# One-hot preparation in pinned half steps, comparisons on other slots, and a sum moved to ScalarE, in an FNet and PEER kernel

## The chip, the cores and the metric

The kernel runs on one core of a Trainium2 chip. A core has a matmul engine (TensorE, PE in the profile), three engines for elementwise work (VectorE or DVE, ScalarE or ACT, GpSimd or POOL), and SyncE (SP), whose queue issues most of the DMA transfers here. The metric is the device time of one launch in microseconds (us), the median of several runs.

## The reference

The reference normalizes the rows of `x` (2048 tokens of 512 numbers), and adds to `x` two functions of the normalized `xn`: a real-valued 2D Fourier transform, and a mixture of tiny experts (PEER) with 32 heads, of which each picks 2 of 4096 experts for each token.

```python
a = jnp.einsum("bsd,ed->bse", x, dft_hid_re)
b = jnp.einsum("bsd,ed->bse", x, dft_hid_im)
y = jnp.einsum("ts,bse->bte", dft_seq_re, a) - jnp.einsum("ts,bse->bte", dft_seq_im, b)
...
s1 = jnp.einsum("nhd,ed->nhe", q1, k1)          # q1, q2: halves of xf @ w_q
s2 = jnp.einsum("nhd,ed->nhe", q2, k2)
i1 = jnp.argsort(-s1, axis=-1)[..., :K]         # K = 2, E = 64
i2 = jnp.argsort(-s2, axis=-1)[..., :K]
...
eidx = (i1[..., :, None] * E + i2[..., None, :]).reshape(BS, H, K * K)
...                                             # best 2 of the 4 candidates: top_s, top_e
g = _softmax(top_s, axis=-1)
ue = u[top_e]
ve = v[top_e]
act = _gelu(jnp.einsum("nd,nhkd->nhk", xf, ue))
out = jnp.einsum("nhk,nhk,nhkd->nd", g, act, ve)
...
return x + _A_ref(xn, ...) + _B_ref(xn, ...)
```

## The kernel before

The first 406 us hold the Fourier transform, the scores of the heads and their routing (the two best keys of each half, the gates). The change touches nothing of that. The DFT matrices are inputs, and the kernel uses their symmetry; so it also checks in passing that the matrices given have it. The second part works on all 4096 experts, without a gather, for 16 blocks of 128 tokens. For each block `b` there are four kinds of work:

- `z`: the matmuls of `xn` with all rows of `u`. Two blocks at a time are computed by a scheme in the manner of Strassen (28 slots of matmuls, L1186), for which VectorE adds partial results out of PSUM (L1227, L1235, L1238) and ScalarE copies others and applies the gelu (L1215), into the block's `act`. Four PSUM banks (`z`) rotate; TensorE waits for an add when it needs the bank. A z phase has 16 slots of the plan (below). The matrices of the scheme come in part from a ring of loads `s` (L1169).
- `g`: the gates spread to a 128 x 4096 table, as matmuls of one-hot matrices (`g_mm`). A step `g{b}_{tg}` (four to a block) has two halves of 16 matmuls of 128x32 (L1289). Each half needs an L (L1279, a comparison with `is_equal`, 128x2048) and an R (L1284, 128x512, then multiplied by the gates on L1287), all on VectorE. Three pairs of buffers L and R rotate, so an L waits until the matmuls three halves earlier are done.
- `W`: `w_part` multiplies `act` by `g` on VectorE (L1297), ScalarE casts the product to 16 bits (L1304; in some steps VectorE does that, L1302), and VectorE subtracts to get the low part (L1305).
- `v`: the matmuls of these weights with the rows of `v` (L1349), in 8 slots `cg` of 12 matmul groups a block; then the sum with the rest of the output `y` (L1364).

The order of the phases is z0, z1, v0, z2+z3, v1, v2, z4+z5, v3, v4 and so on to z14+z15, v13, v14, v15. A plan, filled by `put(phase, cg, ...)`, says behind which slot of a phase the pieces of `g` (`G`), `W`, and the checks are written into the program. A scheduler then orders the instructions of each engine by its own estimate of the time. Only `pin` (`tc.keep_in_program_order`) fixes an instruction behind all that was written earlier for its engine.

The check of the DFT matrices has 64 units `compare` and 4 `compare_w` (tiles `cx`). A unit passes through three successive steps `U`: SP loads a block in two transfers (L1377, L1378); in the next step VectorE sums the first 128x128 block (L1385) and compares the rest with it (L1391 to L1424); in the step after that ScalarE sums the magnitudes of the differences (L1430). Steps `F` do the same with sums alone (`fit`, L1488, L1496, L1500). The tiles `cx`, `fit` and the products of `W` share four buffers.

Of the kernel before, what the change touches and what calls it, by code (L numbers as in the profile page):

```python
# [36 lines left out]
def tile_fnet_peer(ctx, tc, x, ca, cb, c5, wt, wf, wr, wq, kt, ut, vn, out):  # L37
# [9 lines left out]
    nc = tc.nc  # L47
# [46 lines left out]
    chk, asum = sums_sb[:, 0:71], sums_sb[:, 71:139]  # L94
# [201 lines left out]
    G = (1, 0, 2, 3)  # L296
# [424 lines left out]
    def part_b(safe, stS, stP, stQ, stE, xt, u_sb, cmp_p, w4):  # L721
# [370 lines left out]
        def compact_d(b):  # L1092
            compact(b, z_d[b], cmp_p, f"cmp{b % 2}")
# [164 lines left out]
            return work, middle, behind  # L1258

        GP = {}  # L1260

        def parts(b):

            act = ACT[b]
            return act.rearrange("p c n -> p (c n)").bitcast(F16).rearrange(
                "p (c n l) -> p c n l", c=NC, l=2)

        def g_mm(b, tg):
            cmp = CMP[b]
            p = pg(f"g{b}_{tg}")  # L1270
            for hf in range(2):
                ts = slice(tg * TG + hf * 16, tg * TG + hf * 16 + 16)

                def bc(w, n):
                    return cmp[:, w, ts, :].unsqueeze(2).to_broadcast([P, 16, n // 2, 2])

                LR.append(LR.pop(0))
                L, R = LR[-1]
                nc.vector.tensor_tensor(  # L1279
                    L.rearrange("p t (l two) -> p t l two", two=2),  # L1280
                    io_lam.rearrange("p (l two) -> p l two", two=2).unsqueeze(1).to_broadcast([P, 16, P // 2, 2]),
                    bc(0, P), op=ALU.is_equal)
                Rv = R.rearrange("p t (c two) -> p t c two", two=2)
                nc.vector.tensor_tensor(  # L1284
                    Rv, io_c.rearrange("p (c two) -> p c two", two=2).unsqueeze(1).to_broadcast([P, 16, NC // 2, 2]),
                    bc(1, NC), op=ALU.is_equal)
                nc.vector.tensor_tensor(Rv, Rv, bc(2, NC), op=ALU.mult)  # L1287
                for t in range(16):
                    nc.tensor.matmul(p[:, hf, t * NC:(t + 1) * NC], L[:, t, :], R[:, t, :], start=True, stop=True)  # L1289
            GP[b, tg] = p  # L1290

        def w_part(b, tg, here=False):
            act = ACT[b]
            ts = slice(tg * TG, (tg + 1) * TG)
            p = GP.pop((b, tg))
            w = bp.tile([P, NC, TG], F32, tag="w", name=f"w{b}_{tg}", bufs=WB)
# [68 lines left out]
            nc.sync.dma_start(out[b * P:(b + 1) * P], y)  # L1365

        later, loaded = [], []
        pin = tc.keep_in_program_order

        def compare(n):  # L1370

# [9 lines left out]
        def compare_in(n, t, tf, tv):  # L1381

            ri, g, kk = n // 32, n // 8 % 4, n % 8
            odd = kk // 4
            pin(nc.vector.tensor_reduce(asum[:, n:n + 1], tf[:, :P], axis=AX.X, op=ALU.add,  # L1385
                                        apply_absolute_value=True))
            sgn = (((1, 1, 1), (-1, 1, -1)), ((-1, -1, 1), (1, -1, -1)))[ri][odd]
            ops = [ALU.subtract if v > 0 else ALU.add for v in sgn]
            op = ops[1]
            if g == 0:  # L1390
                pin(nc.vector.tensor_tensor(tv[:, 1], tv[:, 1], tv[:, 0], op=ops[0]))  # L1391
                for i in (2, 3):
                    nc.vector.scalar_tensor_tensor(tv[:, i], tv[:, 0], not0, tv[:, i], op0=ALU.mult, op1=ops[i - 1])  # L1393
# [12 lines left out]

            def mirror(v):

                c = 0 if kk else 1
                nc.vector.tensor_tensor(v[:, 2:4, c:], v[:, 2:4, c:], v[:, 0:2, c:], op=m)  # L1410
                if c:
                    nc.vector.tensor_tensor(v[:, 3, 0:1], v[:, 3, 0:1], v[:, 2, 0:1], op=m)

            if g == 0:
                mirror(t[0:1, 2])
                if odd and ri:

                    nc.vector.tensor_copy(t[0:1, 2, 0:2], t[0:1, 0, 0:2])
# [11 lines left out]
            later.append(lambda: pin(nc.scalar.activation(tf[:, P:], tf[:, P:], AF.Abs, accum_out=chk[:, n:n + 1])))  # L1430
# [138 lines left out]
        def pg(name):  # L1569
            return psg.tile([P, 2, 512], F32, tag="pg", name=name, bufs=2)  # L1570
# [21 lines left out]
        F = [U(it=it) for it in fit_units]
        U = U()
# [10 lines left out]
        for b in range(NT):  # L1604
            ph = ("v", b)
            if b % 2 == 0 and 0 < b < 13:
                nx = phases[phases.index(ph) + 1]
                st = 1 if len(nx) == 2 else 2
                put(ph, 1, G(b + 1, 0))
                put(ph, 3, G(b + 1, 1))  # L1610
                put(ph, 5, W(b + 1, 0))
                put(ph, 7, W(b + 1, 1), G(b + 1, 2))
                put(nx, st, W(b + 1, 2, True), G(b + 1, 3))
                put(nx, 3 * st, W(b + 1, 3, True))
            elif b + 1 < NT:
                for k in range(4):
                    put(ph, 2 * k or b % 2, W(b + 1, k))
                put(ph, b % 2, G(b + 1, 2))
                put(ph, 3, G(b + 1, 3))
        put(("v", 13), 5, G(15, 0))  # L1620
        put(("v", 13), 7, G(15, 1))
        for ph in phases[2:]:
            if ph[0] == "z":
                put(ph, 9, G(ph[1], 0))
                put(ph, 12, G(ph[1], 1))
        for b in range(13):
            put(("v", b), 3, lambda b=b: compact_d(b + 2))
        put(("z", 14, 15), 8, lambda: compact_d(15))
        if not safe:
            for cg in (1, 3, 5, 7):  # L1630
                put(("v", 0), cg, F[0])
            for ph, cg in ((("v", 12), 0), (("v", 14), 1), (("v", 14), 3), (("v", 14), 7)):
                put(ph, cg, F[0])
            for ph in phases[3:]:
                if ph[0] == "z":
                    put(ph, 8, F[0])
                    for cg in {2: (9, 11, 13, 15), 4: (9, 11, 13, 15), 6: (9, 11, 13, 15), 14: (9, 12)}.get(ph[1], (9, 12, 15)):
                        put(ph, cg, U)
                elif ph[1] < 14:
                    for cg, f in enumerate((None, F[1], F[1], U, U, U, U, F[0]) if ph[1] % 2 == 0 else (  # L1640
                            None, F[1], F[0], None, U, U, U, F[0])):
                        if f and (ph[1] < 13 or f != U):
                            put(ph, cg, f)
            for cg in range(3):
                put(("v", 14), cg, F[1])
                put(("v", 14 + cg // 2), (6, 7, 0)[cg], U)
                put(("v", 15), cg, F[1])
            for f, n in ((U, 68), (F[0], NK + 16 - V2), (F[1], 16 + V2)):
                assert sum(v.count(f) for v in plan.values()) >= n
# [14 lines left out]
        for n, ph in enumerate(phases):  # L1664
            if ph[0] == "z":
                b = ph[1:]
# [14 lines left out]
            b = ph[1]  # L1681
# [52 lines left out]
    with tc.If(rv > 0):  # L1734
        with tc.tile_pool(name="gen", bufs=1) as gp, \
# [22 lines left out]
            for q in range(4):  # L1758
                ya = gp.tile([P, 4, D], F32, tag="ya", name=f"gya{q}")
                for ri in range(2):  # L1760
                    pp = [gps.tile([P, 512], F32, tag="gp", name=f"gp{q}{ri}{d}", bufs=4)
                          for d in range(KD)]
                    for i in range(NT):
                        t = gp.tile([P, 512], F32, tag="c", name=f"gc{q}{ri}{i}", bufs=2)
                        g, sq = divmod(i, 4)
# [20 lines left out]
                    for a in range(4):  # L1786
                        py = pb(f"gy{q}{ri}{a}")
                        n = 0
# [9 lines left out]
                        b = 4 * a + q  # L1798
# [55 lines left out]
```

## Time and profile before

| what | value |
|---|---|
| median of 3 runs | 1133.58 us (1131.81 to 1138.43) |
| the profiled execution | 1135.25 us, of which the profile's span is 1133.4 |
| TensorE busy | 1107.3 us (98%), granted clock 0.995 of full speed |
| VectorE busy | 962.7 us (85%) |
| ScalarE busy | 663.9 us (59%) |
| GpSimd busy | 332.7 us (29%), nearly all of it ahead of 406 us |

A row of the profile gives the start, the duration, the engine, the line of the kernel and the operation, and then what it writes and reads. In brackets stands how long the engine was idle before the instruction and what ended that idle time.

### The profile page before, as it was taken

The numbers are of one execution on the slowest core, as the hardware profiler recorded it, in microseconds if no ns is written. First come the engines' busy times: TensorE is split into PE (matmuls) and PEld (weight loads), VectorE is DVE, ScalarE is ACT, GpSimd is POOL, SyncE is SP. The second block draws the span as 40 slices with busy tenths as digits, with TensorE's granted clock in tenths as the row PEclk, the third lists the DMA queues.
The fourth block names the chain that finished last, engine by engine and source line by source line (L and its number), as shares of the span: only waits on it lengthen the run. The fifth ranks groups of instructions, "written<-read, shape, count | busy, mean of one in ns | idle before, by whom it ended". The sixth has DMA issues, their size and how long they took to land.

```text
span 1133.4 us, 29112 instructions
## 1 busy us (share of the span) xinstructions
PE 1107.3 (98%) x11528; PEld 722.5 (64%) x11528; DVE 962.7 (85%) x2904; ACT 663.9 (59%) x1098; POOL 332.7 (29%) x385
## 2 busy tenths in 40 slices
PE   9999999999999999999999999999999999999997
PEld 6455554544545459687488478478569569569643
DVE  7899789999989799948997897898888888888793
ACT  6558598888877584346445545544535545544442
POOL 0429999899888850000000000000000000000000
PEclk9999999999999999999999999999999999999999
DMA  9883546465353335866666777666668668566354
GB/s 291 292 206 148 185 139 223 117 217 170 92 168 96 111 108 191 236 199 205 226 206 226 227 218 241 218 207 232 200 205 263 199 211 269 190 221 206 121 168 134
DMA packets 132273, 220.51 MB, mean 195 GB/s; under 512 B 35092, under 2 KB 71067, under 8 KB 132126
## 3 DMA queue, kind: packets, MB, share of 16 engines
q1 hardware_dynamic: 129520, 214.28, 58.7%
q0 software_dynamic: 2304, 4.20, 2.8%
q8 instruction: 92, 1.51, 0.5%
q14 instruction: 55, 0.45, 0.1%
q10 hardware_dynamic: 302, 0.08, 0.0%
HBM read 183.06 MB, written 29.69 MB: 188 GB/s over the span
## 4 chain that ended last, share of the span: by engine, by line
PE 59%; DVE 15%; DMA 5%; ACT 4%; issue 2%; POOL 1%; SPq 0%; ACTq 0%; DVEq 0%
PE s L252 18%; PE z L1186 17%; PE v L1349 16%; PE z L1108 4%; DMA cx<-in_cb_dram 3%; DVE w L1297 3%; DVE L L1279 3%; PE g L1289 3%; DVE act L1305 2%; PE m L148 1%; DVE R L1287 1%; DVE R L1284 1%; DVE w L1305 1%; DMA s<-s_d 1%; DVE cx L1393 1%
## 5 line engine op out<-in xcount | busy, mean ns | idle before, releaser
L252 PE MATMUL s<-m,xq 128*128 128x512 f16 x1344 | 297.4, 379 | 1.7 <-ACT ss L962 1.4
L1349 PE MATMUL v<-v,act 128*128 128x512 f16 x1044 | 233.3, 379 | 0.0
L252 PEld LDWEIGHTS <-xq 128*128 128x128 f16 x1344 | 129.6, 98 | 153.1 <-issue 3.2
L1360 POOL DMA_DIRECT2D y<-in_x_dram x16 | 14.4, 897 | 658.7 <-DMA v<-v_d 274.7
L1279 DVE TENSOR_TENSOR L<-io_lam,cmp 128x2048 f16<-128x2048 f16 x128 | 156.2, 1221 | 28.1 <-PE g L1289 28.1
L1349 PEld LDWEIGHTS <-act 128*128 128x128 f16 x1044 | 99.2, 98 | 112.4
L1186 PEld LDWEIGHTS <-u 128*128 128x128 f16 x2688 | 156.2, 98 | 14.8 <-issue 8.3
L966 DVE MAX8 vals<-ss 128x8 f32<-128x64 f32 x896 | 133.3, 216 | 5.5 <-ACT ss L962 5.2
L1186 PEld LDWEIGHTS <-s 128*128 128x128 f16 x1944 | 110.6, 98 | 1.2 <-DMA s<-s_d 1.2
L1349 PE MATMUL v<-v,w 128*128 128x512 f16 x480 | 109.0, 384 | 0.0
L1304 ACT ACTIVATE act<-w 128x1024 f16<-128x1024 f32 x36 | 48.9, 1358 | 92.2 <-DVE w L1297 92.2
L970 DVE FIND_INDEX8 idx<-vals,ss 128x8 uint16<-128x256 f32 x224 | 93.7, 418 | 0.0
L962 ACT ACTIVATE ss<-s,wsc 128x512 f32<-128x512 f32 x120 | 80.0, 680 | 22.5 <-PE s L252 12.6
L1186 PE MATMUL z<-xb,u 128*128 128x128 f16 x1344 | 84.9, 220 | 5.3 <-DVE w L1227 4.7
L1186 PE MATMUL z<-x,u 128*128 128x128 f16 x1344 | 84.7, 220 | 1.6 <-DVE act L1238 1.1
L1186 PE MATMUL z<-x,s 128*128 128x128 f16 x1296 | 81.2, 219 | 1.0 <-DMA s<-s_d 1.0
L1215 ACT ACTIVATE act<-act,scl 128x512 f32<-128x512 f32 x56 | 39.6, 720 | 70.9 <-DVE act L1235 40.9
L1349 PEld LDWEIGHTS <-w 128*128 128x128 f16 x480 | 46.1, 99 | 53.1 <-issue 2.3
L1430 ACT ACTIVATE cx<-cx 128x896 f32<-128x896 f32 x64 | 60.0, 938 | 29.6 <-DVE cx L1410 11.7
L1289 PEld LDWEIGHTS <-L 128*128 128x128 f16 x2048 | 60.7, 96 | 17.3 <-issue 7.2
L1289 PE MATMUL g<-R,L 128*128 128x32 f16 x2048 | 63.5, 177 | 6.6 <-DVE R L1287 6.2
L1305 DVE TENSOR_TENSOR act<-w,act 128x1024 f16<-128x1024 f32 x44 | 58.6, 1332 | 6.1 <-ACT act L1304 6.1
(363 smaller groups left out, 1878.9 us busy)
## 6 DMA issues: line engine op xcount, KB each, us to landing
v<-v_d SPq DMA_DIRECT2D x67, 512.0 KB, 4.6
s<-s_d SPq DMA_DIRECT2D x63, 512.0 KB, 4.2
cx<-in_cb_dram SPq DMA_DIRECT2D x64, 448.0 KB, 5.7
w<-in_wq_dram SPq DMA_DIRECT2D x28, 512.0 KB, 5.9
fit<-in_wq_dram SPq DMA_DIRECT2D x28, 512.0 KB, 4.3
uv<-in_vn_dram SPq DMA_DIRECT2D x16, 512.0 KB
uv<-in_ut_dram SPq DMA_DIRECT2D x16, 512.0 KB, 3.5
s_d<-v SPq DMA_DIRECT2D x32, 256.0 KB, 2.5
```

Of the source, the lines that this page charges most:

```text
L252: nc.tensor.matmul(ps, xt[i][:, l, kd, :], m[:, r, kd, :], start=(n == 0), stop=(n == 3 * KD - 1))
L962: nc.scalar.activation(s, ps, AF.Copy, scale=inv)
L966: nc.vector.max(vals[:, i, w, :, h], s[:, g, :])
L970: nc.vector.max_index(idx[:, i, w].rearrange("p k h -> p (k h)"), vals[:, i, w, 0:2].rearrange("p k h -> p (k h)"), s[:, w * HC:g + 1, :]. ...
L1108: nc.tensor.matmul(ps if n == 1 else ps.rearrange("p (b n) -> p b n", b=2), ug[:, l, c % 2, kd, :], xb2[:, k0, r, kd, :] if n == 1 else xb ...
L1186: nc.tensor.matmul(bank[:, t * P:(t + 1) * P], lt, rt, start=(t == k == 0 and op in "125"), stop=(t == 3 and k == 5), skip_group_check=op ...
L1279: nc.vector.tensor_tensor(L.rearrange("p t (l two) -> p t l two", two=2), io_lam.rearrange("p (l two) -> p l two", two=2).unsqueeze(1).to_ ...
L1289: nc.tensor.matmul(p[:, hf, t * NC:(t + 1) * NC], L[:, t, :], R[:, t, :], start=True, stop=True)
L1304: nc.scalar.activation(w16[..., 0], w, AF.Copy)
L1305: nc.vector.tensor_tensor(w16[..., 1], w, w16[..., 0], op=ALU.subtract)
L1349: nc.tensor.matmul(pv, w16[:, c, :, l], v_sb[g][:, r, cc, :], start=(n + cc == 0 and k == 0), stop=(n == end and cc == 1 and k == 2))
L1430: later.append(lambda: pin(nc.scalar.activation(tf[:, P:], tf[:, P:], AF.Abs, accum_out=chk[:, n:n + 1])))
```

## The change

The diff does three things. First, the preparation of L and R leaves `g_mm` and becomes `g_prep`, which the plan calls by halves (`LRP`) in slots ahead of the matmuls; L is pinned, R and its product with the gates aren't. Second, the units `U` and `F` get other slots: in z they move from the second half of the phase to slots 0, 4 and (in z2, z4 and z6) 14, with one more in the even v phases; an `F` goes from slot 8 of z to slot 0 of the even v. The number of units stays. Third, the sum of the first block of each `cx` (the reduce on L1385) becomes a ScalarE instruction behind the unit's Abs sum, and is not pinned.

```diff
-        def g_mm(b, tg):
+        def g_prep(b, tg, hfs=(0, 1)):
             cmp = CMP[b]
-            p = pg(f"g{b}_{tg}")
-            for hf in range(2):
+            for hf in hfs:
...
                 L, R = LR[-1]
-                nc.vector.tensor_tensor(
+                PREP.setdefault((b, tg), []).append((L, R))
+                pin(nc.vector.tensor_tensor(
                     L.rearrange("p t (l two) -> p t l two", two=2),
                     io_lam.rearrange("p (l two) -> p l two", two=2).unsqueeze(1).to_broadcast([P, 16, P // 2, 2]),
-                    bc(0, P), op=ALU.is_equal)
+                    bc(0, P), op=ALU.is_equal))
...
+        def g_mm(b, tg):
+            if (b, tg) not in PREP:
+                g_prep(b, tg)
+            p = pg(f"g{b}_{tg}")
+            for hf, (L, R) in enumerate(PREP.pop((b, tg))):
                 for t in range(16):
                     nc.tensor.matmul(p[:, hf, t * NC:(t + 1) * NC], L[:, t, :], R[:, t, :], start=True, stop=True)
...
-            pin(nc.vector.tensor_reduce(asum[:, n:n + 1], tf[:, :P], axis=AX.X, op=ALU.add,
-                                        apply_absolute_value=True))
...
-            later.append(lambda: pin(nc.scalar.activation(tf[:, P:], tf[:, P:], AF.Abs, accum_out=chk[:, n:n + 1])))
+            def sums_abs():
+                pin(nc.scalar.activation(tf[:, P:], tf[:, P:], AF.Abs, accum_out=chk[:, n:n + 1]))
+                nc.scalar.activation(tf[:, :P], tf[:, :P], AF.Abs, accum_out=asum[:, n:n + 1])
+
+            later.append(sums_abs)
...
-                put(ph, 1, G(b + 1, 0))
+                put(("v", b - 1), 7, LRP(b + 1, 0))
+                put(ph, 1, G(b + 1, 0), LRP(b + 1, 1, 0))
+                put(ph, 2, LRP(b + 1, 1, 1))
...
-                put(ph, b % 2, G(b + 1, 2))
+                put(ph, b % 2, G(b + 1, 2), LRP(b + 1, 3, 0))
+                put(ph, b % 2 + 1, LRP(b + 1, 3, 1))
                 put(ph, 3, G(b + 1, 3))
...
-                    put(ph, 8, F[0])
-                    for cg in {2: (9, 11, 13, 15), 4: (9, 11, 13, 15), 6: (9, 11, 13, 15), 14: (9, 12)}.get(ph[1], (9, 12, 15)):
+                    for cg in (0, 4, 14) if ph[1] < 8 else (0, 4):
                         put(ph, cg, U)
                 elif ph[1] < 14:
-                    for cg, f in enumerate((None, F[1], F[1], U, U, U, U, F[0]) if ph[1] % 2 == 0 else (
-                            None, F[1], F[0], None, U, U, U, F[0])):
-                        if f and (ph[1] < 13 or f != U):
-                            put(ph, cg, f)
+                    for cg, fs in enumerate(((F[0],), (F[1],), (F[1], U), (U,), (U,), (U,), (U,), (F[0],)) if ph[1] % 2 == 0 else (
+                            (), (F[1],), (F[0],), (), (U,), (U,), (U,), (F[0],))):
+                        put(ph, cg, *[f for f in fs if ph[1] < 13 or f != U])
```

Three places show what this does to the queues. In the rows below, a tile's first number is its block (in `L0`, `R1` the buffer pair; `cmp3` means that the one-hots are of block 3), and the last number only tells copies apart. The lines 1283, 1288, 1291, 1299, 1307, 1314, 1315 of the new kernel are 1279, 1284, 1287, 1289, 1297, 1304, 1305 of the old one.

VectorE at the end of v1, ahead of the matmuls `g3_0` at the head of v2, before (cx5 and cx6 are comparisons):

```order
L1410 TENSOR_TENSOR cx5_8169<-cx5_8169 1x128
L1385 TENSOR_REDUCE sums_87<-cx6_8196 128x1
L1391 TENSOR_TENSOR cx6_8196<-cx6_8196 128x256
L1393 SCALAR_TENSOR_TENSOR cx6_8196<-cx6_8196,not0_79 128x256 x2
L1287 TENSOR_TENSOR R0_5773<-R0_5773,cmp3_8128 128x512
L1395 TENSOR_TENSOR cx6_8196<-cx6_8196 1x256
L1410 TENSOR_TENSOR cx6_8196<-cx6_8196 128x128
L1410 TENSOR_TENSOR cx6_8196<-cx6_8196 1x128
L1364 SCALAR_TENSOR_TENSOR y1_8221<-v1_7941,scl_93,y1_8221 128x512
L1279 TENSOR_TENSOR L1_5774<-io_lam_72,cmp3_8128 128x2048
L1284 TENSOR_TENSOR R1_5775<-io_c_73,cmp3_8128 128x512
L1279 TENSOR_TENSOR L2_5776<-io_lam_72,cmp3_8128 128x2048
```

And after:

```order
L1417 TENSOR_TENSOR cx3_8131<-cx3_8131 1x128
L1283 TENSOR_TENSOR L1_5774<-io_lam_72,cmp3_8113 128x2048
L1431 TENSOR_TENSOR cx3_8131<-cx3_8131,c52_239 1x128
L1315 TENSOR_TENSOR w4_126<-w2_3_8169,w4_126 128x32x32
L1398 TENSOR_TENSOR cx4_8154<-cx4_8154 128x256
L1400 SCALAR_TENSOR_TENSOR cx4_8154<-cx4_8154,not0_79 128x256 x2
L1291 TENSOR_TENSOR R1_5775<-R1_5775,cmp3_8113 128x512
L1402 TENSOR_TENSOR cx4_8154<-cx4_8154 1x256
L1417 TENSOR_TENSOR cx4_8154<-cx4_8154 128x128
L1417 TENSOR_TENSOR cx4_8154<-cx4_8154 1x128
L1283 TENSOR_TENSOR L0_5772<-io_lam_72,cmp3_8113 128x2048
L1398 TENSOR_TENSOR cx5_8181<-cx5_8181 128x256
```

Both L of block 3 moved from behind the last comparison and the sum `y` to between the comparisons.

VectorE in v7, where the products `w8_0` to `w8_2` of the next block are made and its last `g` is prepared, before:

```order
L1297 SCALAR_TENSOR_TENSOR w8_0_12285<-w4_126,scl_93,g8_0_11890 128x1024
L1305 TENSOR_TENSOR w4_126<-w8_0_12285,w4_126 128x32x32
L1297 SCALAR_TENSOR_TENSOR w8_1_12352<-w4_126,scl_93,g8_1_12065 128x1024
L1279 TENSOR_TENSOR L2_5776<-io_lam_72,cmp8_11216 128x2048
L1284 TENSOR_TENSOR R2_5777<-io_c_73,cmp8_11216 128x512
L1305 TENSOR_TENSOR w4_126<-w8_1_12352,w4_126 128x32x32
L1287 TENSOR_TENSOR R2_5777<-R2_5777,cmp8_11216 128x512
L1297 SCALAR_TENSOR_TENSOR w8_2_12428<-w4_126,scl_93,g8_2_12289 128x1024
```

And after:

```order
L1307 SCALAR_TENSOR_TENSOR w8_0_12276<-w4_126,scl_93,g8_0_11907 128x1024
L1307 SCALAR_TENSOR_TENSOR w8_1_12340<-w4_126,scl_93,g8_1_12078 128x1024
L1315 TENSOR_TENSOR w4_126<-w8_0_12276,w4_126 128x32x32
L1283 TENSOR_TENSOR L1_5774<-io_lam_72,cmp8_11211 128x2048
L1315 TENSOR_TENSOR w4_126<-w8_1_12340,w4_126 128x32x32
L1283 TENSOR_TENSOR L2_5776<-io_lam_72,cmp8_11211 128x2048
L1288 TENSOR_TENSOR R2_5777<-io_c_73,cmp8_11211 128x512
L1307 SCALAR_TENSOR_TENSOR w8_2_12414<-w4_126,scl_93,g8_2_12280 128x1024
L1291 TENSOR_TENSOR R2_5777<-R2_5777,cmp8_11211 128x512
```

The second product stands ahead of the first subtraction now, and a second L and the third product stand ahead of the product of R and the gates (L1291). ScalarE at the same place, after (the casts of `w8_0` to `w8_2`, and sums of `cx` and `fit`):

```order
L1511 ACTIVATE fit38_12324,sums_87<-u9_136 128x1024
L1314 ACTIVATE w4_126<-w8_0_12276 128x32x32
L1438 ACTIVATE cx33_11499,sums_87<-cx33_11499 128x896
L1314 ACTIVATE w4_126<-w8_1_12340 128x32x32
L1438 ACTIVATE cx34_11707,sums_87<-cx34_11707 128x896
```

Before, a sum `fit38` stood between the two casts beside that of the `cx`; it stands ahead of them now.

VectorE in the second half of z8+z9, where the adds out of `z5_8_3`, `z1_8_3` and `z2_8_2` stand, before:

```order
L1235 TENSOR_TENSOR act9_11437<-z5_8_3_11615,act9_11437 128x4x128
L1393 SCALAR_TENSOR_TENSOR cx33_11930<-cx33_11930,not0_79 128x256 x2
L1395 TENSOR_TENSOR cx33_11930<-cx33_11930 1x256
L1238 TENSOR_TENSOR act9_11437<-z1_8_3_11466,w4_126 128x4x128
L1410 TENSOR_TENSOR cx33_11930<-cx33_11930 1x128
L1227 TENSOR_TENSOR w4_126<-z2_8_2_11780,w4_126 128x4x128
```

And after:

```order
L1400 SCALAR_TENSOR_TENSOR cx34_11707<-cx34_11707,not0_79 128x256
L1291 TENSOR_TENSOR R0_5773<-R0_5773,cmp8_11211 128x512
L1400 SCALAR_TENSOR_TENSOR cx34_11707<-cx34_11707,not0_79 128x256
L1402 TENSOR_TENSOR cx34_11707<-cx34_11707 1x256
L1417 TENSOR_TENSOR cx34_11707<-cx34_11707 1x128
L1235 TENSOR_TENSOR act9_11439<-z5_8_3_11619,act9_11439 128x4x128
L1238 TENSOR_TENSOR act9_11439<-z1_8_3_11468,w4_126 128x4x128
L1227 TENSOR_TENSOR w4_126<-z2_8_2_11800,w4_126 128x4x128
```

The comparison moved from between the adds to ahead of all three.

More of the change, by code (lines that the diff above doesn't have):

```diff
@@ L1260, in part_b @@
         GP = {}
+        pin = tc.keep_in_program_order
         def parts(b):
@@ L1266, in parts @@
                 "p (c n l) -> p c n l", c=NC, l=2)
-        def g_mm(b, tg):
+        PREP = {}
+        def g_prep(b, tg, hfs=(0, 1)):
             cmp = CMP[b]
-            p = pg(f"g{b}_{tg}")
-            for hf in range(2):
+            for hf in hfs:
+                assert all(k == (b, tg) for k in PREP) and len(PREP.get((b, tg), ())) == hf
                 ts = slice(tg * TG + hf * 16, tg * TG + hf * 16 + 16)
@@ L1367, in part_b @@
         later, loaded = [], []
-        pin = tc.keep_in_program_order
         def compare(n):
@@ L1584, in G, with LRP @@
             return lambda: g_mm(b, k)
+        def LRP(b, k, *hf):
+            return lambda: g_prep(b, k, hf or (0, 1))
         def W(b, k, here=False):
@@ L1608, in part_b @@
                 st = 1 if len(nx) == 2 else 2
-                put(ph, 1, G(b + 1, 0))
+                put(("v", b - 1), 7, LRP(b + 1, 0))
+                put(ph, 1, G(b + 1, 0), LRP(b + 1, 1, 0))
+                put(ph, 2, LRP(b + 1, 1, 1))
                 put(ph, 3, G(b + 1, 1))
-                put(ph, 5, W(b + 1, 0))
-                put(ph, 7, W(b + 1, 1), G(b + 1, 2))
+                put(ph, 4, LRP(b + 1, 2, 0))
+                put(ph, 5, W(b + 1, 0), LRP(b + 1, 2, 1))
+                put(ph, 7, W(b + 1, 1), G(b + 1, 2), LRP(b + 1, 3, 0))
+                put(nx, 0, LRP(b + 1, 3, 1))
                 put(nx, st, W(b + 1, 2, True), G(b + 1, 3))
@@ L1623, in part_b @@
             if ph[0] == "z":
-                put(ph, 9, G(ph[1], 0))
+                put(ph, 6, LRP(ph[1], 0))
+                put(ph, 9, G(ph[1], 0), LRP(ph[1], 1, 0))
+                put(ph, 10, LRP(ph[1], 1, 1))
                 put(ph, 12, G(ph[1], 1))
+                put(ph, 13, LRP(ph[1], 2, 0))
+                put(ph, 14, LRP(ph[1], 2, 1))
         for b in range(13):
@@ L1631, in part_b @@
                 put(("v", 0), cg, F[0])
-            for ph, cg in ((("v", 12), 0), (("v", 14), 1), (("v", 14), 3), (("v", 14), 7)):
+            for ph, cg in ((("v", 12), 0), (("v", 14), 1), (("v", 14), 3), (("v", 14), 5), (("v", 14), 7)):
                 put(ph, cg, F[0])
```

## The prediction, made before the changed kernel ran

> **What bounds the kernel now.** I read the page first, then the waits of TensorE from 406 us on (the diff touches nothing earlier), then the timeline around each long wait.
>
> ```profile
> span 1133.4 us, 29112 instructions
> PE 1107.3 (98%) x11528; PEld 722.5 (64%) x11528; DVE 962.7 (85%) x2904; ACT 663.9 (59%) x1098; POOL 332.7 (29%) x385
> ```
>
> TensorE (PE) is busy for 98% of the span, and no matmul is removed. So the change can only win back what TensorE waits in this part, and what a lowered clock costs it behind a wait. These are all the waits there (us in total, times, longest):
>
> ```profile
> PE g L1289 <- DVE R L1287: 6.2, 10, 2.2
> PE z L1186 <- DVE w L1227: 4.7, 3, 2.4
> PE z L1186 <- DVE act L1238: 1.1, 1, 1.1
> PE z L1186 <- DMA s<-s_d: 1.0, 1, 1.0
> PE s L252 <- ACT ss L962: 0.9, 1, 0.9
> PE z L1186 <- DVE act L1235: 0.6, 2, 0.3
> PE z L1186 <- DVE act L1227: 0.3, 1, 0.3
> PE z L1186 <- DVE w L1235: 0.2, 1, 0.2
> ```
>
> Without the 0.9 of `s`, which lies ahead of the change, this is 14.1 us, and 13.1 of them end on VectorE (DVE). The `g` waits end on the last of the three one-hot instructions, the `z` waits on the adds that empty a PSUM bank. VectorE isn't full there; it is late at certain places, because its queue holds things in an unlucky order. Three places show how. First, at the head of v2 (and in the same way at 820 us in v8) both L of the matmuls `g3_0` stand behind the comparisons:
>
> ```profile
> 555.03 1.20 DVE L1279 TENSOR_TENSOR L<-io_lam,cmp 128x2048 f16<-128x2048 f16 x1
> 556.50 1.21 DVE L1279 TENSOR_TENSOR L<-io_lam,cmp 128x2048 f16<-128x2048 f16 x1
> 557.63 0.41 DVE L1287 TENSOR_TENSOR R<-R,cmp 128x512 f16<-128x512 f16 x1
> ...
> 558.09 0.55 PE L1289 MATMUL g<-R,L 128*128 128x32 f16 x16 [1.81 <-DVE R L1287]
> 823.02 0.55 PE L1289 MATMUL g<-R,L 128*128 128x32 f16 x16 [2.24 <-DVE R L1287]
> ```
>
> Second, in the second half of a z phase VectorE sits on a comparison whose load is late, with an add of z queued behind it for which TensorE waits:
>
> ```profile
> 773.11 0.88 DVE L1393 SCALAR_TENSOR_TENSOR cx<-cx,not 128x256 f32<-128x256 f32 x2 [2.08 <-DMA cx<-in_cb_dram]
> 775.17 0.67 DVE L1227 TENSOR_TENSOR w<-z,w 128x512 f32<-128x512 f32 x1
> 775.89 1.50 PE L1186 MATMUL z<-xb,u 128*128 128x128 f16 x24 [1.97 <-DVE w L1227]
> ...
> 1040.15 2.19 PE L1186 MATMUL z<-xb,u 128*128 128x128 f16 x24 [2.40 <-DVE w L1227]
> ```
>
> Third, each odd v phase has a small wait at the second half of its `g` matmuls; it is taken up below. Two waits cost more than their length. Windows of 3 us show the granted clock (ahead of the DMA share and GB/s):
>
> ```profile
> 558.00:561.00 3.00, 2.91 (x25) 1.42 (x25) 2.96 (x6) 0.69 (x2) 0.00 (x0) 0.75 0.86 270
> 561.00:564.00 3.00, 3.00 (x11) 1.17 (x10) 2.38 (x7) 0.00 (x0) 0.00 (x0) 0.68 0.96 374
> 823.00:826.00 3.00, 2.98 (x28) 1.57 (x28) 2.97 (x5) 1.27 (x4) 0.00 (x0) 1.00 0.62 179
> 1040.00:1043.00 3.00, 2.85 (x55) 2.85 (x55) 0.68 (x3) 2.31 (x5) 0.00 (x0) 0.63 0.25 100
> 1043.00:1046.00 3.00, 3.00 (x52) 3.00 (x49) 3.00 (x6) 1.70 (x3) 0.00 (x0) 0.80 0.00 0
> ```
>
> Behind the wait of 1.81 us the lost clock is 3 x 0.25 + 3 x 0.32 = 1.7 us, behind that of 2.40 it is 3 x 0.37 + 3 x 0.20 = 1.7, and behind that of 2.24 nothing. So a wait of this length costs the clock in two cases of three. The Trainium skill ("TensorE: Matmul & The Clock Gate", section "Why this matters for your kernels") asks only that gaps over about 3 us be avoided. By that rule neither place would have lost clock; these rows disagree with it, and by the rule alone the sum below would be -4.0 us instead of -6.3.
>
> **The change, part by part.** The durations are from the profiled execution, which took 1135.25 us (span 1133.4 and 1.85 around it); it is 1.67 above the median of the three runs, 1133.58. A difference found in its trace is taken off the median.
>
> *L ahead of its matmuls, pinned, by halves.* The instructions stay the same in number; only their places move. At `g3_0` one L now stands inside the first of the three comparisons there and one behind the second, with R and R*gate among them. From the landing of the first comparison's load on, the new order holds 9.0 us of work up to the last L. The deadline is the first half of `g3_0`, due 0.55 ahead of 558.09 - 1.81, at 555.73: 10.1 us after that landing, if the load comes as late as it did (545.67, first row below).
>
> ```profile
> 545.67 0.43 DVE L1391 TENSOR_TENSOR cx<-cx 128x256 f32<-128x256 f32 x1 [1.83 <-DMA cx<-in_cb_dram]
> ...
> 550.72 0.26 DVE L1385 TENSOR_REDUCE sums<-cx 128x1 f32<-128x128 f32 x1
> 550.91 0.40 DVE L1391 TENSOR_TENSOR cx<-cx 128x256 f32<-128x256 f32 x1
> ```
>
> That removes 1.81 + 1.7 (clock) and, in v8, 2.24: -5.75. If the margin of 1.1 us fails, up to half of it stays.
>
> *The odd v phases.* Here the new order is worse. This is v7 before (the fit sums between the casts left out):
>
> ```profile
> 796.06 1.28 DVE L1297 SCALAR_TENSOR_TENSOR w<-w,scl,g 128x1024 f32<-128x1024 f32 x1 [1.52 <-ACT w L1215]
> 797.37 1.35 ACT L1304 ACTIVATE w<-w 128x1024 f16<-128x1024 f32 x1 [1.35 <-DVE w L1297]
> 798.75 1.31 DVE L1305 TENSOR_TENSOR w<-w,w 128x1024 f16<-128x1024 f32 x1 [1.42 <-ACT w L1304]
> ...
> 803.64 1.20 PE L1289 MATMUL g<-R,L 128*128 128x32 f16 x32
> 803.83 0.40 DVE L1287 TENSOR_TENSOR R<-R,cmp 128x512 f16<-128x512 f16 x1
> ```
>
> VectorE idles 1.42 us for the cast, and R*gate ends at 804.23, just after TensorE wants it at 804.1 (the wait is 0.09). In the new order the second product W stands in that gap, but two L, one R and a third W stand ahead of R*gate. Starting from the same 796.06: W, W (to 798.5), subtraction when the first cast is done (798.75 to 799.95), L (1.13, to 801.08), the second subtraction (its cast can run from 799.6, behind one Abs sum, to 800.95; to 802.28), L (803.42), R (803.75), W (804.94), R*gate (805.3). The matmuls now stand 3 v matmuls, 0.65 us, later, so they are due at 804.7: a wait of 0.6. If the cast stands straight behind the first, it is 0.5; if a fit sum (1.04 us, row below) still lies between, it is 1.5. I take 0.75, near the low end since the ScalarE order shown with the change has one Abs sum between the casts. Seven such phases: 7 x 0.75 = 5.25, less what they wait now. That is the g total of 6.2 without 1.81, 2.24 and some 1.1 at the start and end of the part, or about 1.05. So +4.2, between +2.5 and +9.5.
>
> *The comparisons spread anew.* 68 units stay 68; the units at the second half of z go to its slots 0 and 4 (14 in three phases) and to one more slot of the even v. Each unit's two loads go with it in SP's queue. The waits on L1227, L1235 and L1238 total 6.9. The one at 529.25 (1.1) goes: no comparison waits for a load there any more. Of the other 5.8 I keep 3.0, a wait of about 1 us each at three places where a comparison still stands ahead of an add (start of z2, middle of z8, and z14, where the check's last sum also stands there): -2.8, between 0 and -5.8. The clock behind 1040.15 goes in half the cases, so -0.6 of its 1.7 after allowing for the wait that stays.
>
> *Sums on ScalarE (ACT).* Removed from VectorE are 64 reduces, and 64 Abs sums of 128 elements with their reads are added to ScalarE:
>
> ```profile
> L1385 DVE TENSOR_REDUCE sums<-cx 128x1 f32<-128x128 f32 x64 | 17.8, 277 | 3.9 <-DMA cx<-in_ca_dram 3.9
> L1430 ACT ACTIVATE cx<-cx 128x896 f32<-128x896 f32 x64 | 60.0, 938 | 29.6 <-DVE cx L1410 11.7 <-DVE cx L1418 8.1 <-issue 5.8
> L1430 ACT ACTIVATION_READ_ACCUMULATOR cx<-cx 128x1 f32 x64 | 12.1, 189 | 0.0
> L1488 ACT ACTIVATE fit<-fit 128x1024 f32<-128x1024 f32 x28 | 29.3, 1045 | 0.0
> 417.00:1124.00 707.00, 692.49 (x9041) 508.06 (x9039) 586.06 (x1080) 351.14 (x553) 19.66 (x20) 1.00 0.66 209
> ```
>
> 128 elements more cost 107 ns (1045 against 938), so 128 elements alone take 938 - 6 x 107 = 296 ns, and with the read 485: 31 us more for ScalarE, which is busy 351 of 707 us here. I price this at nothing; the idle half of ScalarE covers it. Without that cover each sum delays a cast, and the subtraction behind it, by 0.5 us. On VectorE a reduce moves the next start by 0.19 (550.72 to 550.91), 12 us in all; it counts only at the places above and is in their sums.
>
> *Start and end.* The first two blocks' `g` come 0.2 later and the end of v14 0.4 earlier by the same addition of rows: -0.2.
>
> **Sum:** -5.75 + 4.2 - 1.1 - 2.8 - 0.6 - 0.2 = -6.25, which gives 1127.3 us.
>
> **Rivals.**
> *The waits go altogether.* If the odd phases keep their 1 us and all other waits on VectorE vanish, 13.1 - 1 and the 3.4 of clock are won: 15.5, or 1118 us. For it: VectorE has 121 idle us in the window row above. Against it: the row sums of the odd phases.
>
> *ScalarE becomes late.* Its 31 us arrive just where casts and bank copies run; a fit sum or an Abs sum of 0.5 between two casts takes the odd phases to 1.5 us each (+5.25 against the forecast): 1132.5, no change. For it, VectorE already idles for a cast (1.42 above). Against it, ScalarE's idle half. The Trainium skill ("ScalarE: Activation LUTs", section "Rules for kernel authors") puts simple arithmetic on VectorE rather than ScalarE. The prices here agree with it (485 ns for 277), and this is the case in which that rule would decide.
>
> *Slower: SP's queue.* SP issues strictly in order. The two loads of a unit at slots 0 and 4 of z now stand among the loads of the `s` ring, each waiting for a free buffer, and the ring has no slack:
>
> ```profile
> 855.78 0.32 SPq L1169 DMA_DIRECT2D s<-s_d  x1
> 859.76 0.33 SPq L1377 DMA_DIRECT2D cx<-in_ca_dram  x1
> 860.67 1.96 SPq L1169 DMA_DIRECT2D s<-s_d  x2
> ```
>
> TensorE's one wait on `s` (1.0) is here, at 860.75. If each of the six z phases from z4 on lost what a late comparison load cost above (2.08), the time would be 1127.3 + 12.5 = 1139.8; it decides from 2.0 us a phase. Against it: by the old row times the buffer comes free some 3.5 us before the ring load behind it could be issued.
>
> **How the numbers follow.** The forecast has 0.48, for 1123.5 to 1131; all waits gone 0.18; ScalarE late 0.17; SP's queue 0.17. Half a per cent, 5.7 us, is about what this kernel's runs tell from no change. Of the forecast's range about 0.6 lies below 1127.9: 0.30 + 0.18 = 0.48 faster; 0.18 + 0.16 = 0.34 same; 0.18 slower. The range reaches down to the case of all waits gone and up into the last, to 1137.
>
> **What would show it.** Right: no wait over 1 us at the heads of v2 and v8, full clock behind them; R*gate last at 0.5 to 1.5 us in the odd v; the z waits on VectorE down to about 3 us; ScalarE busy near 695 us. Wrong: waits on `s` in z, odd-phase waits over 1.5 us, or new waits on pinned L.

## The result, and the profile after

| | before | changed |
|---|---|---|
| median | 1132.69 us (4 runs) | 1149.03 us (4 runs, 1143.74 to 1150.65; a fifth took 1148.01) |
| the profiled execution | 1135.25, span 1133.4, clock 0.995 | 1143.74, span 1141.9, clock 0.996 |

The ratio is 1.0129 (95% interval 1.0086 to 1.0172): the change made the kernel slower by 1.3%, where 1127.3 us had been forecast. The profiled execution is the fastest of the changed kernel's five; the other four ran at a granted clock of 0.991 to 0.994, this one at 0.996.

First the page of the changed kernel, then its waits of TensorE from 406 us on:

```profile
span 1141.9 us, 29279 instructions
PE 1107.5 (97%) x11528; PEld 722.9 (63%) x11528; DVE 951.5 (83%) x2840; ACT 685.0 (60%) x1226; POOL 332.6 (29%) x385
```

```profile
PE z L1186 <- DVE w L1227: 5.5, 3, 2.8
PE g L1299 <- DVE R L1291: 5.1, 8, 1.0
PE z L1186 <- DVE act L1227: 4.7, 3, 2.6
PE z L1186 <- DMA s<-s_d: 4.7, 5, 1.7
PE v L1359 <- DMA v<-v_d: 0.9, 1, 0.9
PE s L252 <- ACT ss L962: 0.9, 1, 0.9
PE g L1299 <- DVE L L1283: 0.8, 2, 0.6
PE z L1186 <- DVE act L1235: 0.3, 1, 0.3
PE z L1186 <- DVE w L1235: 0.2, 1, 0.2
```

Without the 0.9 of the scores' `s` (L252) these are 22.2 us against 14.1: 8.1 more, and the span is 8.5 longer. VectorE works 11 us less and is more often late. The large waits on `R` are gone; in their place stand six waits on L1227, the first add of a z phase (10.2 us; before there were 5.0 in four, most of it in the second half of z), and five on the ring `s` (4.7, before 1.0).

Two of the three places that the prediction showed, now. At the head of v2 the g matmuls run without a wait:

```profile
557.02 0.95 PE L1299 MATMUL g<-R,L 128*128 128x32 f16 x32
```

The third place, the second half of z, has no wait on L1227 left. In v7 the order counted out in advance runs as counted, with a wait of 0.55 at its end:

```profile
805.78 1.31 DVE L1315 TENSOR_TENSOR w<-w,w 128x1024 f16<-128x1024 f32 x1 [0.23 <-ACT w L1314]
806.98 1.21 DVE L1283 TENSOR_TENSOR L<-io_lam,cmp 128x2048 f16<-128x2048 f16 x1
808.11 1.30 DVE L1315 TENSOR_TENSOR w<-w,w 128x1024 f16<-128x1024 f32 x1
809.31 1.21 DVE L1283 TENSOR_TENSOR L<-io_lam,cmp 128x2048 f16<-128x2048 f16 x1
810.43 0.42 DVE L1288 TENSOR_TENSOR R<-io_c,cmp 128x512 f16<-128x512 f16 x1
810.77 1.28 DVE L1307 SCALAR_TENSOR_TENSOR w<-w,scl,g 128x1024 f32<-128x1024 f32 x1
811.96 0.42 DVE L1291 TENSOR_TENSOR R<-R,cmp 128x512 f16<-128x512 f16 x1
...
812.43 0.55 PE L1299 MATMUL g<-R,L 128*128 128x32 f16 x16 [0.55 <-DVE R L1291]
```

The new loss is at the start of the z phases. This is z4, with VectorE from the even v2 on, SP's load for the first comparison there, and the load of `y` ahead of it. First before:

```profile
556.05 0.49 SPq L1377 DMA_DIRECT2D cx<-in_ca_dram  x1
...
562.59 0.43 DVE L1391 TENSOR_TENSOR cx<-cx 128x256 f32<-128x256 f32 x1 [0.62 <-DMA cx<-in_cb_dram]
...
580.81 0.69 DVE L1227 TENSOR_TENSOR act<-z,act 128x512 f32<-128x512 f32 x1 [0.66 <-PE z L1186]
```

And after:

```profile
557.47 0.32 SPq L1369 DMA_DIRECT2D y<-y_d  x1
558.37 0.37 SPq L1386 DMA_DIRECT2D cx<-in_ca_dram  x1
...
564.83 0.42 DVE L1398 TENSOR_TENSOR cx<-cx 128x256 f32<-128x256 f32 x1 [4.53 <-DMA cx<-in_ca_dram]
...
580.60 0.98 DVE L1411 TENSOR_TENSOR cx<-cx 128x768 f32<-128x768 f32 x1
581.47 0.77 DVE L1374 SCALAR_TENSOR_TENSOR y<-v,scl,y 128x512 f32<-128x512 f32 x1
582.13 0.31 DVE L1417 TENSOR_TENSOR cx<-cx 128x128 f32<-128x128 f32 x1
582.33 0.71 DVE L1227 TENSOR_TENSOR act<-z,act 128x512 f32<-128x512 f32 x1
583.09 2.72 PE L1186 MATMUL z<-xb,u 128*128 128x128 f16 x24 [2.61 <-DVE act L1227]
```

VectorE idles 4.53 us at the pinned comparison. Its load is issued 2.3 us later than before (558.37 against 556.05), and VectorE gets there 1.7 us earlier (at 560.30 against 561.97). In SP's queue the load now stands behind the load of `y` (557.47); before, that one came after it (558.69). Then five comparisons instead of four have to fit into the rest of v2. Before, VectorE waited 0.66 us for TensorE at the first add of z4; now TensorE waits 2.61 us for this add.

Two of the six waits also lower the clock behind them, as windows of 3 us behind the waits of 2.61 and 2.77 us (z8) show (granted clock 0.50 and 0.60):

```profile
583.00:586.00 3.00, 2.91 (x28) 2.91 (x28) 3.00 (x6) 1.21 (x2) 0.00 (x0) 0.50 0.92 361
763.00:766.00 3.00, 2.67 (x28) 2.67 (x28) 3.00 (x5) 1.21 (x2) 0.00 (x0) 0.60 0.52 143
```

With the 3 us after these windows (0.98 and 0.83) the lost clock is 1.6 and 1.7 us, about as much as the 1.7 and 1.7 that two waits cost before.

### The profile page after: what moved, and what is told of

The parts are those of the page before. It is cut to its first block, busy times and chain, and to the rows that moved or that the text cites. A ratio compares the mean times of both kernels' runs of the same rounds, so it can differ in the third digit from the quotient of the medians.

```text
span 1141.9 us, 29279 instructions
## 1 busy us (share of the span) xinstructions
PE 1107.5 (97%) x11528; PEld 722.9 (63%) x11528; DVE 951.5 (83%) x2840; ACT 685.0 (60%) x1226; POOL 332.6 (29%) x385
## 4 chain that ended last, share of the span: by engine, by line
PE 48%; DVE 21%; DMA 13%; ACT 7%; POOL 5%; issue 5%; SPq 1%; DVEq 0%; ACTq 0%; POOLq 0%
PE s L252 20%; PE z L1186 15%; PE v L1359 4%; DVE L L1283 4%; DVE w L1307 4%; DMA cx<-in_cb_dram 4%; PE z L1108 3%; ACT act L1314 2%; DVE cx L1411 2%; PE p L449 2%; DVE act L1315 2%; DMA s<-s_d 2%; PE g L1299 2%; DMA y<-in_x_dram 1%; DMA cx<-in_ca_dram 1%
## 5 line engine op out<-in xcount | busy, mean ns | idle before, releaser
L252 PE MATMUL s<-m,xq 128*128 128x512 f16 x1344 | 297.6, 379 | 1.7 <-ACT ss L962 1.4
L252 PEld LDWEIGHTS <-xq 128*128 128x128 f16 x1344 | 129.7, 98 | 153.1 <-issue 3.4
L1370 POOL DMA_DIRECT2D y<-in_x_dram x16 | 14.4, 898 | 663.8 <-DMA y<-y_d 437.8
L1186 PE MATMUL z<-xb,u 128*128 128x128 f16 x1344 | 86.4, 222 | 10.2 <-DVE w L1227 5.5
L1307 DVE SCALAR_TENSOR_TENSOR w<-act,scl,g 128x1024 f32<-128x1024 f32 x44 | 55.6, 1277 | 12.9 <-ACT act L1215 12.9
```

The costliest lines, as they stand in the source:

```text
L252: nc.tensor.matmul(ps, xt[i][:, l, kd, :], m[:, r, kd, :], start=(n == 0), stop=(n == 3 * KD - 1))
L1186: nc.tensor.matmul(bank[:, t * P:(t + 1) * P], lt, rt, start=(t == k == 0 and op in "125"), stop=(t == 3 and k == 5), skip_group_check=op ...
L1307: nc.vector.scalar_tensor_tensor(w, act[:, :, ts], fw, p.rearrange("p h (n c) -> p c (h n)", c=NC), op0=ALU.mult, op1=ALU.mult)
```

## The experiments

All ratios are to the kernel before on the same chip, with the 95% interval. "Waits" are TensorE's from 406 us on without `s` of the scores, in the profiled execution (14.1 before, 22.2 changed).

| kernel | median us | ratio | waits |
|---|---|---|---|
| new slots alone | 1146.89 | 1.0137 (1.0101 to 1.0173) | 25.9 |
| one-hot steps alone | 1137.28 | 1.0045 (1.0021 to 1.0069) | 17.4 |
| sums on ScalarE alone | 1127.13 | 0.9959 (0.9935 to 0.9984) | 6.8 |
| all but the new slots | 1130.67 | 0.9992 (0.9973 to 1.0010) | 11.9 |
| z slots 0, 4, 9, 14, no fifth | 1140.49 | 1.0085 (1.0053 to 1.0116) | 18.4 |
| fifth comparison in even v alone | 1143.17 | 1.0085 (1.0055 to 1.0116) | 18.9 |
| fit sum moved alone | 1134.01 | 1.0017 (0.9991 to 1.0043) | 13.2 |
| changed, z slots 2 and 5 | 1152.18 | 1.0178 (1.0151 to 1.0204) | 25.8 |
| sum on VectorE, not pinned | 1143.59 | 1.0109 (1.0079 to 1.0140) | 17.9 |
| sum on VectorE, twice | 1132.18 | 1.0005 (0.9985 to 1.0025) | 12.2 |
| sums on ScalarE, each twice | 1123.42 | 0.9908 (0.9875 to 0.9941) | 9.4 |
| all but the slots, odd-v L not pinned | 1134.57 | 1.0015 (0.9997 to 1.0032) | 14.4 |
| sums on ScalarE, earlier loads | 1130.48 | 0.9967 (0.9947 to 0.9988) | 12.1 |

**The three parts, each by itself.** The new slots alone:

```diff
-                    put(ph, 8, F[0])
-                    for cg in {2: (9, 11, 13, 15), 4: (9, 11, 13, 15), 6: (9, 11, 13, 15), 14: (9, 12)}.get(ph[1], (9, 12, 15)):
+                    for cg in (0, 4, 14) if ph[1] < 8 else (0, 4):
```

(and the even v's list of the change, with the fit sum there).

> The kernel before with the new slots of the comparisons and fit sums alone (one-hots and the sum of the first block as before). Theory A (the new slots cause the loss: the even v phases get a fifth comparison whose load comes late, VectorE reaches the start of z with a backlog, and the ring loads stand behind comparison loads in SP's queue): slower than before by 7 to 16 us, waits on L1227 at the starts of z together over 6 us, waits on the ring s over 3 us. Theory B (the sums on ScalarE hold the buffers longer, so that loads come late): within 3 us of before. Theory C (the pinned L hold up VectorE): within 3 us of before.

Slower by 1.4%, as much as the whole change. The waits on L1227 are 7.1 + 5.6, all seven at the start of a z phase, those on `s` 3.1. Theory A holds in its numbers; B and C are out.

The one-hots alone (`g_prep`, `LRP`, the pinned L):

> The kernel before with the pinned half steps of the one-hots alone. Theory A: the heads of v2 and v8 lose their waits, the odd v phases wait 0.6 to 0.8 each; in all 0 to 4 us faster than before, with no wait over 1 us on L1227 at the start of a z phase. Theory B: the same. Theory C: slower by 5 us or more, with VectorE idle at pinned L ahead of adds.

All theories missed. The heads of v2 and v8 are cured and six of the seven odd v wait 0.66 to 0.77, but the kernel is 0.45% slower, neither a gain nor 5 us clear. Its largest waits of TensorE say where:

```profile
PE g L1299 <- DVE R L1291: 4.5, 7, 0.8
PE z L1186 <- DVE act L1238: 3.3, 2, 2.1
PE z L1186 <- DVE w L1227: 3.3, 3, 1.4
PE z L1186 <- DVE act L1227: 2.5, 1, 2.5
PE z L1186 <- DVE w L1235: 1.9, 1, 1.9
PE z L1186 <- ACT act L1232: 1.1, 1, 1.1
```

The adds of z are late, in part at places where nothing was before: L1238 3.3 (1.1 before), L1235 1.9, and ScalarE's copy on L1232 1.1.

The sums on ScalarE alone (the reduce deleted, `sums_abs` added):

> The kernel before with the sums of the first blocks on ScalarE alone. Theory A: within 3 us of before; VectorE's busy time falls by some 18 us and nothing else changes much. Theory B: slower by 5 us or more, with loads of comparisons issued 0.5 us or more later and waits on them longer. Theory C: within 3 us.

Faster by 0.4%, some 5 us (1.8 to 7.4 by the interval). Theory B is refuted; A and C, within 3 us, aren't excluded by the interval, but neither named a gain. Half of the waits are gone in the profiled execution, which is the fastest of ten (1123.62 us), and no wait in it lowers the clock. All waits of TensorE left from 406 us on:

```profile
PE z L1186 <- DVE w L1227: 3.6, 3, 1.5
PE z L1186 <- DVE act L1238: 1.5, 1, 1.5
PE g L1289 <- DVE R L1287: 1.2, 2, 1.0
PE s L252 <- ACT ss L962: 0.9, 1, 0.9
PE z L1186 <- DVE act L1235: 0.5, 1, 0.5
```

The waits at the heads of v2 and v8 (1.81 and 2.24) are gone here too, without any change in how one-hots are planned: in this order one L of `g3_0` stands ahead of the comparisons (543.07 us). These two are 4.05 of the 7.3 us by which the waits fell.

The changed kernel with the slots of before:

> The changed kernel with the comparisons and fit sums on their slots of before (one-hots pinned, sums on ScalarE). Theory A: 1 to 6 us faster than before, that is 14 to 22 faster than the changed kernel. Theory B: slower than before by 5 us or more. Theory C: slower than before by 5 us or more.

It agrees with before within 0.2%, 16 us faster than the changed kernel; theory A is right in the difference, and in the absolute number at its weak end, within the noise. B and C are out. The parts taken singly add up: +1.37 + 0.45 - 0.41 = 1.41%, with 1.29 measured.

**What in the new slots costs.** Three kernels take one piece each, the first two together with the moved fit sum: the early z slots (0, 4, 9, 14 up to z6, 0, 4, 9 later, 0, 4 in z14), the fifth comparison of the even v (with z on 9, 12, 15 or 9, 12), the moved fit sum (on slot 0 of the even v, and one more in v14).

```diff
 # early z slots (even v as before)
+                    for cg in (0, 4, 9, 14) if ph[1] < 8 else (0, 4, 9) if ph[1] < 14 else (0, 4):
 # fifth comparison (even v as in the change)
+                    for cg in (9, 12, 15) if ph[1] < 8 else (9, 12):
```

> The kernel before with the comparisons of z on slots 0, 4, 9 and 14 (0, 4, 9 in the later ones) and the fit sum moved from z to the even v, but no fifth comparison in the even v. Theory A1 (the step on slot 0 of z compares a block whose load was issued only at the end of v, and the ring loads stand behind the loads of slots 0 and 4): slower than before by 7 to 16 us, with waits on L1227 at the starts of z of 6 us or more together. Theory A2 (the fifth comparison of the even v makes VectorE late): within 4 us of before.

> The kernel before with the fifth comparison in each even v and one fewer in each z, those of z staying on slots 9, 12, 15. Theory A1: within 4 us of before. Theory A2: slower than before by 7 us or more, and VectorE reaches the starts of z late although nothing stands on slot 0 there.

> The kernel before with only the fit sum moved from slot 8 of z to slot 0 of the even v. Theories A1 and A2: within 3 us of before. A third theory, that the fit's load at the start of the even v takes the buffer that the comparisons' loads wait for: slower by 5 us or more, first comparison load of the even v issued 2 us later.

Both pieces cost 0.85%, the fit sum nothing that can be told. So A1 and A2 were each half right: each piece costs, and neither alone is the loss. Both make the starts of z late. With the fifth comparison the waits on L1227 are 6.6 + 3.7, of which 7.6 at the start of all seven z phases. VectorE in v2 of that kernel:

```profile
566.54 0.43 DVE L1391 TENSOR_TENSOR cx<-cx 128x256 f32<-128x256 f32 x1 [2.18 <-DMA cx<-in_cb_dram]
...
582.97 0.75 DVE L1364 SCALAR_TENSOR_TENSOR y<-v,scl,y 128x512 f32<-128x512 f32 x1
583.63 0.68 DVE L1227 TENSOR_TENSOR act<-z,act 128x512 f32<-128x512 f32 x1
```

With the early z slots alone, 4.9 us of waits on L1227 stand at the starts of three z phases, below the 6 that A1 asked for; the adds on L1235 in the middle of z (6.1 us) and the ring (2.7) are late too. The longest wait on the ring ends, by the profile, with a load issued right behind a comparison's load:

```profile
676.44 0.42 SPq L1378 DMA_DIRECT2D cx<-in_cb_dram  x1
677.24 1.16 SPq L1169 DMA_DIRECT2D s<-s_d  x1
...
687.56 1.51 PE L1186 MATMUL z<-x,s 128*128 128x128 f16 x24 [1.81 <-DMA s<-s_d]
```

By that it took 10.3 us from issue to landing, while the core's DMA engines were busy for 94% or more of the time from 676 to 684 us. Whether the order in SP's queue or the traffic of all these loads made it late was not separated.

Then slot 0 itself, in the changed kernel:

```diff
-                    for cg in (0, 4, 14) if ph[1] < 8 else (0, 4):
+                    for cg in (2, 5, 14) if ph[1] < 8 else (2, 5):
```

> The changed kernel with the comparisons of z on slots 2 and 5 instead of 0 and 4 (14 stays). If the step on slot 0 is what makes the starts of z late: the waits on L1227 at the starts of z fall from 10.2 to under 3 us together, and the kernel is 6 us or more faster than the changed one. If it is the fifth comparison in the even v: only the one at z8 (2.8 us, where the comparison of slot 0 stands ahead of the add) goes, the other five stay, and the kernel is 1 to 5 us faster than the changed one, that is still 10 us or more slower than before.

The wait at z8 fell from 2.77 to 0.65, and of the others at starts of z all but the last stayed or grew (2.2, 2.95, 2.08, 0.73; at z14 0.32 instead of 1.43), much as under the second theory. But the kernel got no faster: TensorE waits 4.9 us for the adds on L1235 instead of 0.5, up to 1.7 each. Both theories missed that.

**What the sums win.** The sum kept on VectorE, without its pin:

```diff
-            pin(nc.vector.tensor_reduce(asum[:, n:n + 1], tf[:, :P], axis=AX.X, op=ALU.add,
+            nc.vector.tensor_reduce(asum[:, n:n + 1], tf[:, :P], axis=AX.X, op=ALU.add,
```

> The kernel before with the sum of the first block still on VectorE, but not pinned. If the gain of the sums on ScalarE comes from the 12 us of VectorE time: within 2 us of before. If it comes from the order (a pinned sum ahead of each comparison that waits for the load): 3 to 7 us faster than before.

It is slower by 1.1%, which neither had. Its group in this kernel, from 406 us on:

```profile
L1385 DVE TENSOR_REDUCE sums<-cx 128x1 f32<-128x128 f32 x64 | 18.1, 284 | 20.0 <-DMA cx<-in_ca_dram 20.0
```

The pinned sum idles 3.9 us for its load, the free one 20.0, and ahead of adds of z: the scheduler puts it earlier than the load comes. The next kernel kept place and pin and cut the size:

```diff
-            pin(nc.vector.tensor_reduce(asum[:, n:n + 1], tf[:, :P], axis=AX.X, op=ALU.add,
+            pin(nc.vector.tensor_reduce(asum[:, n:n + 1], tf[:, :2], axis=AX.X, op=ALU.add,
```

> The kernel before with the pinned sum on VectorE over 2 instead of 128 elements of each row (it leaves out most of that sum); place and pin stay. If the gain of the sums on ScalarE is VectorE's time: faster than before by 2 to 5 us, since some 8 of its 12 us go. If it is the pinned instruction that waits for the first load: within 2 us of before.

It took 1804.56 us. With most of the sum left out, the kernel no longer takes the DFT matrices for symmetric and computes the general way too (13448 matmuls instead of 11528), so it says nothing on the question. The opposite could be run, the same pinned line twice:

> The kernel before with the pinned sum of the first block done twice on VectorE (12 us more of its time in all). If VectorE's time is what the sums on ScalarE win: slower than before by 4 to 8 us. If it is the order or the wait for the first of the two loads: within 2 us of before.

Another 12 us of VectorE's time at the same places cost nothing (1.0005). But most of it fell into time that VectorE had spent waiting: from 406 us on it idles 35.3 us for the comparisons' loads before, 26.7 with the doubled sum and 21.9 with the sums on ScalarE. So this doesn't show that VectorE's time is free everywhere, and less idling for loads alone doesn't make the kernel faster. What points to the order are the heads of v2 and v8: with the doubled sum the L of `g3_0` stand where they stood and waits of 0.61 and 2.51 remain there; with the sums on ScalarE one L moved ahead and both waits went. For the rest of the gain the cause was not isolated, since the doubled line changed the order at other places too.

And the sums on ScalarE, with the line doubled there:

```diff
                 nc.scalar.activation(tf[:, :P], tf[:, :P], AF.Abs, accum_out=asum[:, n:n + 1])
+                nc.scalar.activation(tf[:, :P], tf[:, :P], AF.Abs, accum_out=asum[:, n:n + 1])
```

> The kernel before with the sums on ScalarE, each done twice (31 us more for ScalarE; VectorE's order is the same as with them once). If ScalarE's idle half hides the sums: 3 to 7 us faster than before, as with them once. If they delay casts and the buffers' release: no faster than before, with more waits of VectorE on casts and on the comparisons' loads.

ScalarE's idle half hides the sums, even doubled. VectorE's order is the same in both, so that the sums once and twice can differ only by ScalarE and the clock; their intervals just overlap, and whether the useless second sum helps stays open.

**Two attempts at a better version.** From all but the slots, only the L of `g(b,3)` for even b lose their pin:

```diff
-                pin(nc.vector.tensor_tensor(
+                (pin if tg != 3 or b % 2 else lambda i: i)(nc.vector.tensor_tensor(
```

> The kernel with pinned one-hots and the sums on ScalarE (comparisons on their old slots), in which only the L of the last step g(b,3) of even blocks, which fall in the odd v phases, are not pinned. If the pinned second L is what makes TensorE wait in the odd v (0.55 to 0.63 in seven phases): those waits fall to 0.2 or less, 3 to 5 us faster than with all L pinned, so 5 to 7 us faster than before. If the order of the products and subtractions (two products ahead of the first subtraction) is the cause: the waits stay, no change against all L pinned.

The waits at this place fell to 0.2 or less in three of the seven phases, as under the first theory, and to between 0.35 and 0.42 in the others; yet the kernel is not faster (1.0015 against 0.9992). In the trace new waits stand a little earlier in the same phases, on the add ahead of the last z matmuls. In v7:

```profile
798.56 1.50 PE L1186 MATMUL z<-x,u 128*128 128x128 f16 x24 [1.39 <-DVE act L1238]
```

Waits of 1.0 stand likewise at 623 and 710 us. The lateness moved; it was not removed.

With the sums on ScalarE alone, earlier loads from z8 on:

```diff
-                    put(ph, 8, F[0])
-                    for cg in {2: (9, 11, 13, 15), 4: (9, 11, 13, 15), 6: (9, 11, 13, 15), 14: (9, 12)}.get(ph[1], (9, 12, 15)):
+                    put(ph, 9, F[0])
+                    for cg in {2: (9, 11, 13, 15), 4: (9, 11, 13, 15), 6: (9, 11, 13, 15), 14: (8, 12)}.get(ph[1], (8, 12, 15)):
```

> The kernel before with the sums on ScalarE, and in z8, z10, z12 and z14 the first comparison load one slot earlier (8 instead of 9, the fit sum on 9). If the two waits left on L1227 (771 and 1030 us, 1.5 each) come from loads that arrive late at the comparison on slot 12: they fall below 0.5 each, 6 to 10 us faster than before. If the order around them decides: within 2 us of the sums on ScalarE alone, that is 3 to 7 us faster than before.

The wait at 771 is gone, that at 1030 is now 2.1 at 1035, and new ones on L1235 (1.4, 2.1, 1.1) took their place. As the second theory had it, the time is that of the sums alone: 0.9967 against 0.9959. So the sums on ScalarE alone are a version that beats both kernels, by 0.4% and (by the ratios) 1.7%.

## Why the prediction was wrong, step by step

- **What bounds the kernel** was right: TensorE's waits, most of them on a late VectorE, explain 8.1 of the 8.5 us between the two spans (-4.05 at the heads of v2 and v8, +2.7 in the odd v, +3.8 on the adds of z, +3.7 on the ring, +2.0 at the start and the end). The rest of the 16 us in the medians lies outside the two profiled executions, and is partly clock: the means over all executions are 0.993 changed and 0.995 to 0.996 before, some 2 to 3 us of 1140.
- **L ahead of its matmuls, -5.75:** the two waits (4.05) went as said, with full clock behind them. The clock that was to be won was lost again behind two other waits (3.3 us, 3.4 before). The sums alone remove the two waits too, so in company this step won nothing, and the one-hot steps alone made new waits on the adds of z that the forecast's sum left out (17.4 us of waits against 14.1).
- **The odd v, +4.2:** right in place, somewhat large in size. Seven waits of 0.55 to 0.63 were counted out as 0.6 and taken as 0.75. Before, these phases waited 1.4 us and not 1.05, since the 0.63 at 1076.79 is v13's; so the term measured +2.7.
- **The comparisons spread anew, -4.5 with the clock: this is the step that failed.** Alone it is +14 us. Of the 6.9 us that TensorE waited for VectorE's adds in z it kept 3.0, and there are 10.7 now. It priced the places that the units left, the second half of z, and for their arrival allowed about 1 us at each of three places, of which the start of z2 was one. There were six waits at starts of z, 10.2 us together. Missing were the fifth comparison's time in the even v, where VectorE has to be on time for the first add, and its load, which is issued later while VectorE arrives earlier (4.53 us idle). Its row sums took loads to land when they had landed before.
- **The sums, priced at nothing:** the price of one was right (299 and 188 ns measured against 296 and 189), though ScalarE's busy time rose by 21 us and not by 31, and the price was not the point. The kernel with them alone gained 0.4%, and over half of the fall in its waits is the order at the heads of v2 and v8.
- **Start and end, -0.2:** measured +2.0. Waits of 0.62, 1.00 and, for a load of `v` at 1126 us, 0.95 stand there, where 0.75 in all stood before.
- **The rival on SP's queue** (0.17) happened in part: 4.7 us of waits on `s`, 3.7 more than before, where 12.5 were priced. By the profile three of the five (2.5 us) end with a ring load issued right behind a comparison's load, and the other two, with the longest, behind the load of `y`. The slower time came mainly from a mechanism that no rival had, VectorE late at the starts of z. ScalarE did not become late: no wait of TensorE behind 407 us ends on it. The prices of one sum agree with the Trainium skill's advice to use VectorE and not ScalarE for simple arithmetic ("ScalarE: Activation LUTs", "Rules for kernel authors"): 487 ns against 277. Yet the kernel with the sums on ScalarE is 0.4% faster: here the slower engine, idle for nearly half of this part (379 of 716 us busy in the changed kernel), was the better place.

## What to carry to other kernels

When work is moved to other slots, price the place where it arrives as carefully as the one that it leaves: what is queued behind it there, and whether its load can be there by then. An instruction that waits for a load held up everything behind it on its engine here, so its place mattered more than its duration: a sum of 0.28 us could be doubled for nothing where VectorE waited for a load anyway, while unpinning it cost 1.1%. And try each part of a change by itself: here one of three was worth keeping.

## What was not expected of the hardware

The granted clock differs between executions of one program, and the time with it. The slowest of the changed kernel's five took 1150.65 us at 0.991, the fastest 1143.74 at 0.996: of the 6.9 us, an estimated 0.005 x 1148 = 5.7 are clock. The kernels with more waits had the lower mean clock (0.991 and 0.994 with 26 us of waits, 0.995 to 0.998 with about 12 or less).

Single waits show where it goes. In the 15 profiled executions (the 1804 us run left out), all eight waits of TensorE of 2.5 us and more were followed by a lowered clock, which lost 1.5 to 1.7 us in the 6 us behind them (2.7 behind the one of 5.39). Of the 27 between 1.76 and 2.48 us nine were, with 1.7 us lost each time, and none of the shorter ones was by itself. So a wait of about 2 us costs either its length or nearly double, and in this case that was not to be told in advance.
